# Linear attention and two feed-forward layers on one core: four blocks of the first layer turned into pairs of seven products, PReLU as one maximum, the whole kernel noted as one graph and ordered

## The chip, the cores and the metric

The kernel runs on one core of a Trainium2 chip. The metric is the time of one execution in device microseconds, as the median of several runs. The engines are named as in the profile: PE (TensorE), DVE (VectorE), ACT (ScalarE), POOL (GpSimd) and SP (SyncE, which here only issues DMAs).

## The reference

Linear attention comes first, then a feed-forward layer with PReLU, then one with a sigmoid gelu. All weights of the two feed-forward layers arrive as 64-bit floats and are turned into 32-bit ones on the chip.

```python
kv = np.einsum('bhsd,bhse->bhde', k, v)             # batch 8, heads 8, sequence 576, head size 64
out = np.einsum('bhsd,bhde->bhse', q, kv)
rms = np.sqrt(np.mean(out * out, axis=-1, keepdims=True) + 1e-06)
x = out / rms * g_norm                              # then laid out as 4608 tokens of 512 features
...
h = x @ w_in                                        # first layer: 512 -> 2048
g = np.maximum(h, 0.0) + alpha * np.minimum(h, 0.0)
x = g @ w_out                                       # 2048 -> 512
...
h = x @ w_in                                        # second layer, weights of its own
g = h * (1.0 / (1.0 + np.exp(-1.702 * h)))
return g @ w_out
```

## The kernel before, in words

The 4608 tokens are worked through in nine blocks of 512 tokens (j = 0 to 8). A feed-forward layer has 16 slices of 128 hidden features (m = 0 to 15). Each 32-bit operand is split into a high and a low part, and a product of two operands is three matmuls (high by high, high by low, low by high), each 128 by 128 by 512.

**Plain blocks.** `gemm_in` makes one slice h (12 matmuls), the activation makes g, `split` makes its two parts, and two steps later (`LAG`) `gemm_out` adds the slice to four output tiles y (12 matmuls). So a slice of a block is 24 matmuls and a block 384. All nine blocks of the first layer (l = 0) and block 0 of the second (l = 1) are plain. Blocks 0 and 1 of the first layer take turns, seven slices each first (`MH`), so that the weights have time to arrive; all 32 weight tiles of a layer stay in the on-chip memory.

**Pairs.** Blocks 1 and 2, 3 and 4, 5 and 6, 7 and 8 of the second layer are worked as pairs: two slices by two blocks are four hidden tiles, and a 2 by 2 scheme makes them from seven products instead of eight. A pair takes 7 x 8 = 56 steps (`NS`), and a step has 6 matmuls into the hidden tiles (`pair_in`) and 6 out of them (`pair_out`, 24 steps later, `LAGP`), so a pair is 672 matmuls. The price is sums and differences of blocks on DVE (`factor`), of weights beforehand on POOL (`w2_sums`), and a weight tile of 512 KB loaded from DRAM for each step (`weights`), since the prepared products are stored there.

**Weights.** `stage_words`, `stage_bits` and `stage_split` turn a loaded 64-bit weight into 32 bits (ACT two passes, DVE three, POOL one integer sum) and split it (ACT and DVE). For the second layer the products of two weight tiles at a time (one unit: k and kind, 16 in all) are made, split and stored to DRAM by `w2_steps`.

**Attention** of block j is made of small jobs (`job_kv`, `job_q`, `job_out`, `job_x`), spread by hand between the slices of block j-1. The PReLU reads the hidden tile in PSUM twice on DVE (lines 463 and 466); for seven slices of block 0 ACT makes two parts, and DVE joins them from the on-chip memory (line 459).

**Order.** Up to the pairs the order of instructions is written out by hand: `FIRST`, `ORDER` and `PROLOGUE` for the start, `jobs` by half steps for attention, `PREP` (half steps 44 to 280) for the second layer's weights. The pairs are noted as operations with costs, and `arrange` plays them through on a model and fixes the order on every engine.

Of the kernel before, what the change touches and what calls it, by code (L numbers as in the profile page):

```python
# [9 lines left out]
F32 = mybir.dt.float32  # L10
# [12 lines left out]
RING = 3  # L23
# [8 lines left out]
SEQ = "a0 a1 o0 a2 o1 . x0 o2 a3 x2 . o3 x1 . x3"  # L32

K1 = (0, 4)
J1 = (5, 9)
J2 = (3, 16)

RATE = (1.0, 0.55)


# [4 lines left out]
WA = 6  # L45
# [4 lines left out]
MM, TR, ACT, DVE, ISSUE, LAND, HOP = 0.2268, 0.09, 0.64, 0.71, 0.1, 4.5, 0.2  # L50
AHEAD = {"wt": 8.0, "xs": 20.0, "xc": 80.0, "gr": 8.0}
SLACK = 12.0
SPARE = (50.0, 4)

PREP = (44, 236)
# [4 lines left out]
def linear_attention_two_ffn_kernel(  # L60
# [22 lines left out]

    nc = tc.nc
# [14 lines left out]
    sp = ctx.enter_context(tc.tile_pool(name="small", bufs=2))  # L99

    big = ctx.enter_context(tc.tile_pool(name="big", bufs=1))
    half = ctx.enter_context(tc.tile_pool(name="half", bufs=1))
    n4 = [f"w{i}" for i in range(2 * M)]
    count = {"x": 2 * KC, "ld": RING, "raw": 1, "hl": LAG + 1}
    count2 = {"g": 1, "qT": 2, "xn": 2, "ev": 2, "da": 4, "dr": 2, "kR": 1, "vR": 1, "kv": 2}

    def place(tag, shape, dtype, name):
        if tag in count2:
            return half.tile(shape, dtype, tag=tag, name=name, bufs=count2[tag])
        return big.tile(shape, dtype, tag=tag, name=name, bufs=count.get(tag, 1))  # L110

    dram = ctx.enter_context(tc.tile_pool(name="dram", bufs=1, space=bass.MemoryType.DRAM))
    ps_h = ctx.enter_context(tc.tile_pool(name="ps_h", bufs=2, space=bass.MemoryType.PSUM))
    ps_y = ctx.enter_context(tc.tile_pool(name="ps_y", bufs=1, space=bass.MemoryType.PSUM))
    ps_a = ctx.enter_context(tc.tile_pool(name="ps_a", bufs=2, space=bass.MemoryType.PSUM))
# [3 lines left out]
    nalpha_sb = const.tile([P, M], F32, name="nalpha_sb")  # L119
    g_sb = const.tile([P, 1], F32, name="g_sb")  # L120
    kR = place("kR", [P, H, D], F32, "kR")
    vR = place("vR", [P, H, D], F32, "vR")
    kvb = [place("kv", [P, NP, P], F32, f"kv{i}") for i in range(2)]
# [5 lines left out]
    PAIRS = [(1, j) for j in range(1, NB, 2)]  # L129
    HB = TB // 2  # L130
    w2s = [dram.tile([P, 2, 2, HB], F32, name=f"w2s{u}") for u in range(NS)]
    ws = {1: w2s}
    src_d = {1: x2d}
    w2x = {kind: [dram.tile([P, 2, HB], F32, name=f"w2x{kind}{k}") for k in range(NQ)] for kind in ("wi", "wo")}


    loaded = {}
    queue = deque()

    def load(key, tag="ld"):  # L140
        t = place(tag, [P, 2 * TB], F32, "ld")
        LOAD[key[0]](t, *key[1:])
        loaded[key] = t

    def issue():
        if queue:
            load(queue.popleft())

    def runs(t0, n):
        done = 0  # L150
        while done < n:
            b, s = divmod(t0 + done, S)
            step = min(n - done, S - s)
            yield done, step, b, s
            done += step

    def load_q(t, i0):
        for e in range(2):
            for off, n, b, s in runs((i0 + e) * P, P):
                nc.sync.dma_start(  # L160
                    out=t[off : off + n, e * TB : (e + 1) * TB].rearrange("p (h d) -> p h d", h=H),
                    in_=q[b, :, s : s + n, :].rearrange("h p d -> p h d"),
                )

    def load_q0(t, p):
        for h in range(2):
            nc.sync.dma_start(
                out=t[:, 0:TB].rearrange("p (t h d) -> p t h d", h=2, d=D)[:, :, h, :],
                in_=q[0, 2 * p + h, 0:TB, :].rearrange("(t p) d -> p t d", p=P),
            )  # L170

    def load_kv(t, b, p):
        kt = t[:, 0:TB].rearrange("p (r h d) -> p r h d", r=R, h=2)
        vt = t[:, TB:].rearrange("p (h r d) -> p h r d", r=R, h=2)
        for h in range(2):
            nc.sync.dma_start(  # L176
                out=kt[:, :, h, :], in_=k[b, 2 * p + h, 0:S0, :].rearrange("(p r) d -> p r d", r=R)
            )
        nc.sync.dma_start(
            out=vt, in_=v[b, 2 * p : 2 * p + 2, 0:S0, :].rearrange("h (p r) d -> p h r d", r=R)  # L180
        )

    def load_rest(b):
        for t, src in ((kR, k), (vR, v)):
            nc.sync.dma_start(out=t[0:SR], in_=src[b, :, S0:S, :].rearrange("h p d -> p h d"))

    def load_win(t, l, m):
        nc.sync.dma_start(
            out=t.bitcast(I64).rearrange("p (c f) -> p c f", c=KC),
            in_=(w_in1, w_in2)[l][:, m * P : (m + 1) * P].rearrange("(c p) f -> p c f", p=P),  # L190
        )

    def load_wout(t, l, m):
        nc.sync.dma_start(out=t.bitcast(I64), in_=(w_out1, w_out2)[l][m * P : (m + 1) * P, :])

    def load_yp(t, c):
        nc.sync.dma_start(
            out=t.rearrange("p (c t) -> p c t", c=2), in_=yp[c : c + 2].rearrange("c p t -> p c t")
        )

    def load_x2(t, j, c):
        nc.sync.dma_start(
            out=t.rearrange("p (c t) -> p c t", c=2), in_=x2d[j][c : c + 2].rearrange("c p t -> p c t")
        )

    LOAD = {"q": load_q, "q0": load_q0, "kv": load_kv, "wi": load_win, "wo": load_wout, "x2": load_x2, "yp": load_yp}


    def split(src, hi, lo):
        nc.scalar.activation(out=hi, in_=src, func=AF.Copy)  # L210
        nc.vector.tensor_tensor(out=lo, in0=src, in1=hi.bitcast(F32), op=ALU.subtract)  # L211

    w_t = {}
    dec = {}

    def slot(kind, m):
        return n4[m + (M if kind == "wo" else 0)]

    def load_w(key):
        load(key, slot(key[0], key[2]))

    def stage_words(key):

        t = loaded[key]
        w2 = t.bitcast(U32).rearrange("p (n two) -> p n two", two=2)
        f2 = t.rearrange("p (n two) -> p n two", two=2)
        a = place("da", [P, TB], F32, "da")
        r = place("dr", [P, TB], I32, "dr")  # L230
        nc.scalar.activation(out=a, in_=f2[:, :, 1], func=AF.Abs)
        nc.scalar.activation(out=r, in_=w2[:, :, 0], func=AF.Copy, scale=2.0**-29)
        dec[key] = (a, r, w2[:, :, 1])

    def stage_bits(key):
        a, r, high = dec[key]
        au = a.bitcast(U32)

        nc.vector.tensor_scalar(out=a, in0=a, scalar1=2.0**-15, scalar2=122880.0, op0=ALU.max, op1=ALU.min)
        nc.vector.tensor_scalar(  # L240
            out=au,
            in0=au,
            scalar1=3,
            scalar2=0x3FFFFFF8,
            op0=ALU.logical_shift_left,
            op1=ALU.bitwise_and,
        )
        nc.vector.scalar_tensor_tensor(  # L248
            out=au, in0=high, scalar=0xC0000000, in1=au, op0=ALU.bitwise_and, op1=ALU.bitwise_or
        )  # L250
        ai = a.bitcast(I32)
        nc.gpsimd.tensor_tensor(out=ai, in0=ai, in1=r, op=ALU.add)  # L252

    def stage_split(key):
        a, _, _ = dec.pop(key)
        kind, l, m = key
        t = place(slot(kind, m), [P, 2, TB], F32R, "w")
        loaded.pop(key)
        split(a, t[:, 0, :], t[:, 1, :])
        w_t[key] = t  # L260


    def w2_load(kind, m):
        t = place("raw", [P, 2 * TB], F32, "raw")
        LOAD[kind](t, 1, m)
        loaded[kind, 1, m] = t

    def w2_place(kind, k, p):

        i = PRODUCTS.index(p)  # L270
        if kind == "wi":
            return w2s[k // 2 * 14 + 2 * i + k % 2][:, 0]
        return w2s[(k // SEG * 7 * SEG + i * SEG + k % SEG + LAGP) % NS][:, 1]

    def w2_out(src, dst):
        t = place("ev", [P, 2, HB], F32R, "wsp")
        split(src, t[:, 0, :], t[:, 1, :])
        nc.sync.dma_start(out=dst, in_=t.bitcast(F32))

    def w2_plain(kind, k, e):  # L280
        a = dec[kind, 1, 2 * k + e][0]
        loaded.pop((kind, 1, 2 * k + e))

        names = ((11, 12), (21, 22)) if kind == "wi" else ((11, 21), (12, 22))
        for h in range(2):
            name = names[e][h]
            dst = w2x[kind][k] if name == 21 else w2_place(kind, k, {11: 1, 12: 2, 22: 4}[name])
            w2_out(a[:, h * HB : (h + 1) * HB], dst)
# [835 lines left out]
```

## Time and profile before

| | us |
|---|---|
| median of 3 runs | 1676.7 (1676.02 to 1678.06) |
| the profiled execution | 1676.33 |
| span of its instructions | 1674.6 |
| PE busy in it | 1629.4 |

The profile is one execution. Busy time is that of each engine by itself; PEld is the weight load of PE, which runs beside its matmuls. In the rows by stage the columns are: stretch in us from the start, its length, then the busy time of PE, PEld, DVE, ACT and POOL with the number of instructions in brackets, the granted clock of PE as a share of full speed, the busy share of the DMA engines, and GB/s. The chain is followed back from the last instruction, at each step to what released it.

### The profile page before, as it was taken

How to read it: one execution, taken by the hardware profiler on the slowest of the kernel's cores; microseconds unless marked ns; L12 is line 12 of the kernel's file. 1: busy time of each engine (PE TensorE's matmuls, PEld its weight loads, DVE VectorE, ACT ScalarE, POOL GpSimd, SP SyncE). 2: the span in 40 equal slices, each digit the busy share in tenths (PEclk: the TensorE clock that was granted, in tenths of full speed). 3: DMA queues.
4: the chain of work that ended last, by engine and by line, in shares of the span. 5: the costliest groups of instructions: out<-in, count | busy, mean ns of one | idle time of the engine just before them, and what ended most of it. 6: DMA issues, size and time to landing. Idle time of an engine off the chain costs nothing.

```text
span 1674.6 us, 20949 instructions
## 1 busy us (share of the span) xinstructions
PE 1629.4 (97%) x7584; PEld 1346.5 (80%) x7584; DVE 1013.2 (61%) x1741; ACT 654.6 (39%) x1225; POOL 144.4 (9%) x138
## 2 busy tenths in 40 slices
PE   5889999999999999999999998999999999999998
PEld 4668877888888888888888887888888888888887
DVE  5888665655656566565656313476666648564555
ACT  4554332322322232233332223645455445544543
POOL 1323111110101111111111000000000000000000
PEclk8899999999999999999999999999999999999999
DMA  9750335333353432422238711757666756764752
GB/s 226 205 205 1 76 119 135 94 119 107 101 158 101 123 100 92 133 88 101 88 123 274 234 55 66 279 189 254 198 214 199 245 173 226 245 218 138 288 179 76
DMA packets 200535, 261.44 MB, mean 156 GB/s; under 512 B 92400, under 2 KB 133360, under 8 KB 200432
## 3 DMA queue, kind: packets, MB, share of 16 engines
q1 hardware_dynamic: 200432, 260.11, 48.6%
q8 instruction: 60, 0.98, 0.2%
q14 instruction: 43, 0.35, 0.1%
HBM read 206.58 MB, written 53.48 MB: 155 GB/s over the span
## 4 chain that ended last, share of the span: by engine, by line
PE 87%; DVE 4%; SPq 3%; DMA 2%; ACT 2%; issue 1%; POOL 0%; DVEq 0%; ACTq 0%; POOLq 0%
PE y L485 23%; PE cX L690 10%; PE V L690 10%; PE cZ L690 8%; PE W L690 8%; PE h L449 8%; PE h L451 8%; PE h L450 8%; PE ops L382 2%; SPq L176 1%; PE kvps L348 1%; SPq L160 1%; PE xTps L413 1%; PE oT L862 1%; PE qTps L372 1%
## 5 line engine op out<-in xcount | busy, mean ns | idle before, releaser
L485 PE MATMUL y<-gs,w 128*128 128x512 f32 x1728 | 427.3, 396 | 1.5 <-DVE ev L498 0.8
L485 PEld LDWEIGHTS y<-gs,w 128*128 128x128 f32 x1728 | 319.4, 189 | 68.7 <-DVE ev L498 1.7
L210 ACT ACTIVATE gs<-g 128x512 fp32r<-128x512 f32 x160 | 101.0, 632 | 430.7 <-DVE g L466 418.0
L449 PE MATMUL h<-x,w 128*128 128x512 f32 x640 | 256.3, 401 | 3.8 <-ACT x L415 3.7
L450 PE MATMUL h<-x,w 128*128 128x512 f32 x640 | 251.7, 393 | 0.1
L451 PE MATMUL h<-x,w 128*128 128x512 f32 x640 | 251.7, 393 | 0.0
L211 DVE TENSOR_TENSOR gs<-g,gs 128x512 fp32r<-128x512 f32 x160 | 113.7, 710 | 171.4 <-ACT gs L210 171.4
L690 PE MATMUL cX<-xc,wt 128*128 128x512 f32 x768 | 195.4, 391 | 4.4 <-DMA wt<-w2s 4.4
L690 PE MATMUL V<-gr,wt 128*128 128x512 f32 x768 | 195.6, 391 | 0.0
L690 PEld LDWEIGHTS cX<-xc,wt 128*128 128x128 f32 x768 | 144.9, 189 | 35.2 <-issue 4.8
L690 PEld LDWEIGHTS V<-gr,wt 128*128 128x128 f32 x768 | 142.9, 188 | 28.9
L463 DVE TENSOR_SCALAR g<-h,alpha_sb 128x512 f32<-128x512 f32 x137 | 102.4, 747 | 90.9 <-PE h L451 90.4
L252 POOL TENSOR_TENSOR da<-da,dr 128x512 int32<-128x512 int32 x64 | 91.2, 1425 | 765.6 <-DVE da L248 759.3
L690 PE MATMUL cZ<-xc,wt 128*128 128x512 f32 x576 | 146.5, 391 | 0.0
L690 PE MATMUL W<-gr,wt 128*128 128x512 f32 x576 | 145.1, 390 | 0.8 <-ACT ev L865 0.8
L449 PEld LDWEIGHTS h<-x,w 128*128 128x128 f32 x640 | 121.9, 190 | 28.9 <-ACT x L415 4.1
L451 PEld LDWEIGHTS h<-x,w 128*128 128x128 f32 x640 | 121.5, 190 | 26.0
L450 PEld LDWEIGHTS h<-x,w 128*128 128x128 f32 x640 | 121.9, 190 | 25.4 <-DVE x L416 1.1
L690 PEld LDWEIGHTS cZ<-xc,wt 128*128 128x128 f32 x576 | 109.1, 189 | 22.8
L690 PEld LDWEIGHTS W<-gr,wt 128*128 128x128 f32 x576 | 107.9, 188 | 23.8 <-ACT ev L865 1.5
L760 DVE TENSOR_TENSOR gr<-gt,gr 128x512 fp32r<-128x512 f32 x96 | 65.8, 688 | 56.7 <-ACT gr L756 55.3
L466 DVE SCALAR_TENSOR_TENSOR g<-h,g 128x512 f32<-128x512 f32 x137 | 94.7, 692 | 4.7
(99 smaller groups left out, 1718.8 us busy)
## 6 DMA issues: line engine op xcount, KB each, us to landing
wt<-w2s SPq DMA_DIRECT2D x200, 512.0 KB, 4.3
w2s<-wsp SPq DMA_DIRECT2D x112, 256.0 KB, 2.3
w<-w2s SPq DMA_DIRECT2D x48, 256.0 KB, 5.1
wt<-w2s SPq DMA_DIRECT2D x48, 256.0 KB, 3.8
x2d<-ev SPq DMA_DIRECT2D x36, 256.0 KB, 2.0
out_dram<-ev SPq DMA_DIRECT2D x36, 256.0 KB, 2.1
ld<-in_k_dram SPq DMA_DIRECT2D x64, 128.0 KB, 3.5
ld<-in_v_dram SPq DMA_DIRECT2D x32, 256.0 KB, 3.9
```

What stands on the lines that cost most here:

```text
L210: nc.scalar.activation(out=hi, in_=src, func=AF.Copy)
L211: nc.vector.tensor_tensor(out=lo, in0=src, in1=hi.bitcast(F32), op=ALU.subtract)
L252: nc.gpsimd.tensor_tensor(out=ai, in0=ai, in1=r, op=ALU.add)
L382: nc.tensor.matmul(ps[off : off + n, t], lhsT=qT[:, t * P + off : t * P + off + n], rhs=kvb[b % 2][:, p, :], start=True, stop=True,)
L449: nc.tensor.matmul(ps, lhsT=wh[:, c, :], rhs=x[c][:, 0], start=(c == 0), stop=False)
L450: nc.tensor.matmul(ps, lhsT=wh[:, c, :], rhs=x[c][:, 1], start=False, stop=False)
L451: nc.tensor.matmul(ps, lhsT=wl[:, c, :], rhs=x[c][:, 0], start=False, stop=(c == KC - 1))
L463: nc.vector.tensor_scalar(out=g, in0=ps, scalar1=0.0, scalar2=alpha_sb[:, m : m + 1], op0=ALU.min, op1=ALU.mult)
L466: nc.vector.scalar_tensor_tensor(out=g, in0=ps, scalar=0.0, in1=g, op0=ALU.max, op1=ALU.add)
L485: nc.tensor.matmul(y_t[c], lhsT=a, rhs=b, start=(m == m0 and n == 0), stop=(m == m1 and n == 2))
L690: nc.tensor.matmul(ps, lhsT=x, rhs=y, start=start and n == 0, stop=stop and n == 2, skip_group_check=True)
L760: nc.vector.tensor_tensor(out=t[:, 1], in0=val(), in1=t[:, 0].bitcast(F32), op=ALU.subtract)
```

## The change

- Blocks 5 to 8 of the first layer become two pairs (`run1`), of 56 steps each, with PReLU in place of gelu. Five blocks stay plain (`PLAIN`). The order of stages is: five plain blocks of the first layer, block 0 of the second layer, two pairs of the first layer, four pairs of the second.
- The attention of blocks 3 to 8 is now noted over 16 or 14 half steps each in place of 32 (`JOBS`), so that all of it is noted ahead of the end of block 4. The results of attention for blocks 3 to 8 are stored to DRAM (`xd`) and loaded again.
- The first layer's weights are needed twice: each is stored as 32 bits (`w1f`) when it has been converted, and three of its seven products are stored then; `weights1` loads the 32 bits again, makes the four other products on POOL (`sums`), splits them and stores them.
- PReLU is ACT's copy from PSUM with a sign (1 or -1, by whether alpha is at most 1), and then one instruction on DVE, the maximum of h and alpha times h, from and to the on-chip memory. The sign is multiplied into the second weights of the layer (`wo`).
- In a pair a step's weights come as two loads of 256 KB each (2 KB of each partition) and not as one of 512 KB.
- The hand order is gone. Every operation of the kernel is noted with its engine, cost, tiles and how far ahead it may start, `arrange` is run three times, each time with the PE starts of the run before as due times, and the best order is emitted. The model has POOL as an engine, a rate for the DMAs, and 1.7 times the cost for DVE operations marked `two` while POOL works. There are 45 tiles of 4 KB per partition and 20 of 2 KB for all.

```diff
-RING = 3
-FIRST = "qkrqkkqgwqkawwww"
-ORDER = "rkkkwwkwwqqw"
-PROLOGUE = "q0 k0 q1 o0 k1 o1 x0 q2 k2 o2 W B W k3 B e q3 x1 o3 S x2 W x3 B a W S S"
+FIRST = "q0 k0 q1 o0 k1 o1 x0 q2 k2 o2 k3 q3 x1 o3 x2 x3"
-J1 = (5, 9)
-J2 = (3, 16)
+J1 = (4, 9)
+J2 = (35, 16)
+PLAIN = 5
+JOBS = {3: (64, 16), 4: (80, 16), 5: (96, 16), 6: (112, 16), 7: (128, 14), 8: (142, 14)}
+PLAIN2_FIRST = True
-MM, TR, ACT, DVE, ISSUE, LAND, HOP = 0.2268, 0.09, 0.64, 0.71, 0.1, 4.5, 0.2
-AHEAD = {"wt": 8.0, "xs": 20.0, "xc": 80.0, "gr": 8.0}
-PREP = (44, 236)
+MM, TR, ACT, DVE, POOL, ISSUE, LAND, RATE, HOP = 0.2268, 0.09, 0.64, 0.71, 1.45, 0.65, 2.2, 0.3, 0.2
+AHEAD = {"wt": 10.0, "xs": 20.0, "xc": 80.0, "gr": 8.0, "ld": 14.0, "raw": 45.0, "w2p": 12.0, "x": 15.0}
+PASSES = 3
+RINGS = (6, 2, 3)
+N4, N2 = 45, 20
...
+    xd = {j: dram.tile([KC, P, TB], F32, name=f"xd{j}") for j in range(min(3, PLAIN), NB)}
...
+            if o.eng == "PE":
+                o.late = before[o.n] if before else o.clock
...
+            cost = o.cost
+            if o.two and free_at["POOL"] > t + 0.3:
+                cost *= 1.7
+            start[o.n] = t
+            free_at[o.eng] = t + cost
+            fin[o.n] = t + cost
+            if o.eng == "SP":
+                dma_at = max(dma_at, t + cost) + o.mb / RATE
+                fin[o.n] = dma_at + LAND
...
+    def emit():
+        found = None
+        starts = None
+        for _ in range(PASSES):
+            end, starts, fin = arrange(starts)
+            if found is None or end < found[0]:
+                found = (end, starts, fin)
...
+        for o in sorted(ops, key=lambda o: (starts[o.n], o.n)):
...
+        if j in xd:
+            xo = ("xo", j, p)
...
+                "SP", ISSUE, lambda: nc.sync.dma_start(out=xd[j][p], in_=tl(xo)), reads=[(xo, 0)],
...
+    def weight1(kind, m):
...
+        if kind == "wo":
+            note(
+                "ACT", ACT,
+                lambda: nc.scalar.activation(out=tl(da), in_=tl(da), func=AF.Copy, scale=sign_sb[:, m : m + 1]),
+                reads=[(("alpha",), 0)], writes=[(da, 0)], slack=None,
+            )
+        note_split([(da, 0)], lambda: tl(da), w, "halves", slack=None, held=[held_by[da]])
+        note(
+            "SP", ISSUE, lambda: nc.sync.dma_start(out=w1f[kind][m], in_=tl(da)), reads=[(da, 0), held_by[da]],
+            writes=[(("w1f", kind, m), 0)], slack=25.0, mb=0.26,
+        )
+        for h, pp in (((0, (1, 2)),), ((1, (4,)),))[m % 2] if kind == "wi" else (((0, (1,)),), ((0, (2,)), (1, (4,))))[m % 2]:
+            note(
+                "SP", ISSUE,
+                lambda h=h, pp=pp: nc.sync.dma_start(
+                    out=w_place(0, kind, m // 2, pp),
...
+    def sums(l, kind, k, da):
...
+        def one():
+            a11, a22, a12, a21 = parts()
+            t = tl(s12)
+            nc.gpsimd.tensor_tensor(out=t[:, 1], in0=a21, in1=a22, op=ALU.add)
+            nc.gpsimd.tensor_tensor(out=t[:, 0], in0=t[:, 1], in1=a11, op=ALU.subtract)
...
+        note("POOL", 1.8, one, reads=src, writes=[(s12, 0), t12], new=[(s12, [P, 2, HB], F32, "2")], **kw)
+        note("POOL", 1.8, two, reads=[*src, (s12, 0), t12], writes=[(s34, 0), t34], new=[(s34, [P, 2, HB], F32, "2")], **kw)
+    def weights1():
+        for k in range(NQ):
+            for kind in ("wi", "wo"):
...
+                        lambda da=das[e], src=w1f[kind][m]: nc.sync.dma_start(out=tl(da), in_=src),
...
+                sums(0, kind, k, das)
+    def prelu(o, m):
+        nc.vector.scalar_tensor_tensor(
+            out=o, in0=o, scalar=alpha_sb[:, m : m + 1], in1=o, op0=ALU.mult, op1=ALU.max
+        )
...
         def fn():
-            t = tl(("wt", u)).bitcast(F32)
-            if len(parts) == 2 and parts[0][1] is parts[1][1]:
-                nc.sync.dma_start(out=t, in_=parts[0][1])
-            else:
-                for e, w in parts:
-                    nc.sync.dma_start(out=t[:, e], in_=w[:, e])
+            t = tl(key).bitcast(F32)
+            for e, w in parts:
+                nc.sync.dma_start(out=t[:, e : e + 1], in_=w)
...
+        if not l:
+            note("DVE", DVE, lambda: prelu(val(), m), reads=[h], writes=[h], two=True)
...
-    segs += [(0, j, 0, M - 1) for j in range(2, NB)] + [(1, 0, 0, M - 1)]
+    segs += [(0, j, 0, M - 1) for j in range(2, PLAIN)]
...
+        plain(steps, jobs)
+        for fn in (weights2, weights1) if PLAIN2_FIRST else (weights1, weights2):
+            fn()
+        run1 = [(0, j) for j in range(PLAIN, NB, 2)]
+        run2 = [(1, j) for j in range(1, NB, 2)]
...
+        if PLAIN2_FIRST:
+            plain2()
+            pairs(run1 + run2)
```

## Rows read from the trace of the kernel before

**Rows 1.** The page: span, busy time of engines, chain that ended last.

```profile
span 1674.6 us, 20949 instructions
...
PE 1629.4 (97%) x7584; PEld 1346.5 (80%) x7584; DVE 1013.2 (61%) x1741; ACT 654.6 (39%) x1225; POOL 144.4 (9%) x138
...
PE 87%; DVE 4%; SPq 3%; DMA 2%; ACT 2%; issue 1%; POOL 0%; DVEq 0%; ACTq 0%; POOLq 0%
```

**Rows 2.** Busy time by stage: each engine, granted clock, DMA share, GB/s.

```profile
0.00:32.64 32.64, 17.56 (x104) 15.21 (x105) 15.41 (x39) 14.10 (x33) 5.24 (x12) 0.92 0.98 224
...
32.64:118.67 86.03, 71.16 (x317) 55.10 (x318) 68.33 (x120) 48.22 (x90) 25.06 (x16) 0.89 0.73 218
...
300.00:860.00 560.00, 559.85 (x2729) 465.31 (x2728) 352.23 (x656) 166.82 (x341) 70.97 (x73) 1.00 0.35 106
...
1028.80:1050.00 21.20, 16.78 (x64) 13.41 (x63) 5.58 (x9) 6.29 (x11) 0.00 (x0) 0.84 0.55 191
...
1050.00:1633.00 583.00, 582.23 (x2613) 481.87 (x2612) 354.81 (x554) 295.14 (x526) 0.00 (x0) 1.00 0.64 216
```

**Rows 3.** The chain in order of time: start us, us, what.

```profile
118.67 2.72 PE y L485 x12
...
358.69 2.72 PE y L485 x12
...
658.45 2.72 PE y L485 x12
...
1633.55 5.44 PE W L690 x24
```

**Rows 4.** What PE waited for: us in total, times, longest.

```profile
PE cX L690 <- DMA wt<-w2s: 4.4, 1, 4.4
```

**Rows 5.** Groups by line, DVE, ACT and POOL: busy us, mean ns, idle before.

```profile
L211 DVE TENSOR_TENSOR gs<-g,gs 128x512 fp32r<-128x512 f32 x160 | 113.7, 710 | 171.4 <-ACT gs L210 171.4
...
L463 DVE TENSOR_SCALAR g<-h,alpha_sb 128x512 f32<-128x512 f32 x137 | 102.4, 747 | 90.9 <-PE h L451 90.4
...
L466 DVE SCALAR_TENSOR_TENSOR g<-h,g 128x512 f32<-128x512 f32 x137 | 94.7, 692 | 4.7
...
L239 DVE TENSOR_SCALAR da<-da 128x512 f32<-128x512 f32 x64 | 29.7, 464 | 0.1
...
L240 DVE TENSOR_SCALAR da<-da 128x512 uint32<-128x512 uint32 x64 | 29.2, 457 | 2.2
...
L248 DVE SCALAR_TENSOR_TENSOR da<-raw,da 128x512 uint32<-128x512 uint32 x32 | 22.2, 692 | 1.1
...
L300 POOL TENSOR_TENSOR ws<-da,ws 128x256 f32<-128x256 f32 x16 | 14.0, 873 | 0.0
```

**Rows 6.** Line 459 by itself: duration ns min, median, max.

```profile
L459 DVE SCALAR_TENSOR_TENSOR g<-neg,nalpha_sb,g x7: 752/1528/1786, 39.1 to 99.3; 128x512 f32<-128x512 f32 x7
```

**Rows 7.** DVE in order of time: start us, us.

```profile
77.15 1.79 DVE L459 SCALAR_TENSOR_TENSOR g<-neg,nalpha_sb,g 128x512 f32<-128x512 f32 x1
```

**Rows 8.** POOL in order of time, the same stretch.

```profile
76.78 1.60 POOL L252 TENSOR_TENSOR da<-da,dr 128x512 int32<-128x512 int32 x1 [3.57 <-DVE da L248]
```

**Rows 9.** Busy time by stage again, a stretch of the start and one pair.

```profile
50.00:100.00 50.00, 40.77 (x195) 31.24 (x194) 44.10 (x82) 30.00 (x58) 15.50 (x10) 0.93 0.76 240
...
1100.00:1252.30 152.30, 152.06 (x687) 125.82 (x686) 96.52 (x150) 77.92 (x139) 0.00 (x0) 1.00 0.64 218
```

**Rows 10.** PE groups by line up to 118.67 us: count, busy us, mean ns.

```profile
L485 PE MATMUL y<-gs,w 128*128 128x512 f32 x85 | 21.6, 399 | 0.5 <-DVE w L211 0.5
...
L449 PE MATMUL h<-x,w 128*128 128x512 f32 x40 | 19.3, 483 | 3.8 <-ACT x L415 3.7
```

**Rows 11.** DMA issues: count, KB each, median us to landing.

```profile
w2s<-wsp SPq DMA_DIRECT2D x112, 256.0 KB, 2.3
...
raw<-in_moe_w_in_dram SPq DMA_DIRECT2D x16, 512.0 KB, 4.2
```

**Rows 12.** Tile wsp: its stores, min/median/max ns, first and last start us.

```profile
L278 SPq DMA_DIRECT2D w2s<-wsp x112: 319/338/1227, 230.9 to 928.5; - x112
```

More of the change, by code (lines that the diff above doesn't have):

```diff
@@ L98, in linear_attention_two_ffn_kernel @@
     const = ctx.enter_context(tc.tile_pool(name="const", bufs=1))
[L99 to L110, printed above, removed]
+    sp = ctx.enter_context(tc.tile_pool(name="small", bufs=8))
@@ L132, in linear_attention_two_ffn_kernel @@
[L132 to L155, printed above, removed]
@@ new lines, in arrange @@
+            cost = o.cost
[7 more added lines that the diff above has]
+                fin[o.n] = dma_at + LAND
+            changed = {o.eng}
+            if o.eng == "POOL":
+                changed.add("DVE")
+            for c, k in o.need:
+                del room[c][:k]
+                best.clear()
@@ L662, in pairs @@
-    def pairs():
+                    room[cls[key]].append(ends[key])
+                    room[cls[key]].sort()
+                    best.clear()
+            for a in after[o.n]:
+                left[a.n] -= 1
+                if not left[a.n]:
+                    arrive(a)
+                    changed.add(a.eng)
+            for e in changed:
+                best.pop(e, None)
+        for o in ops:
+            o.end = fin[o.n]
+        return max(s + o.cost for s, o in zip(start, ops) if o.eng == "PE"), start, fin
@@ new lines, in note_split, with part, value @@
+    def note_split(src, val, key, cost, ahead=None, slack=SLACK, low=None, dep=(), held=()):
+        halves = cost == "halves"
+        shape = [P, 2, 2, HB] if halves else [P, 2, TB]
+        def part(i):
+            return tl(key)[:, :, i] if halves else tl(key)[:, i]
+        def value():
+            return val().rearrange("p (h f) -> p h f", h=2) if halves else val()
+        note(
+            "ACT", ACT, lambda: nc.scalar.activation(out=part(0), in_=value(), func=AF.Copy), reads=src,
+            writes=[(key, 0), *dep], new=[(key, shape, F32R, "4")], ahead=ahead, slack=slack, low=low,
+        )
+        note(
+            "DVE", DVE,
+            lambda: nc.vector.tensor_tensor(out=part(1), in0=value(), in1=part(0).bitcast(F32), op=ALU.subtract),
+            reads=[*src, (key, 0), *held], writes=[(key, 1)], slack=slack, two=True,
+        )
@@ L726, in inputs @@
+                writes=[(key, e) for e in range(2)], new=[(key, [P, 2, TB], F32, "4")], ahead=AHEAD["xs"],
+                slack=None, low=SPARE, mb=0.52,
             )
@@ L878, in note_pairs, with pairs @@
+        note(
+            "ACT", ACT, lambda: nc.scalar.copy(tl(ev), tl(bank)), reads=[(bank, 0)], writes=[(ev, 0)],
+            new=[(ev, [P, TB], F32, "2")], slack=4.0,
+        )
+        note("SP", ISSUE, lambda: nc.sync.dma_start(out=out[r0 : r0 + P, :], in_=tl(ev)), reads=[(ev, 0)], mb=0.26)
+    def pairs(run):
+        n_in = len(run) * NS
+        pair_inputs(*run[0])
         for s in range(n_in + LAGP + 4):
             if s < n_in + LAGP:
-                weights(s)
-            if s < n_in and s % NS == NS // 2 and s // NS + 1 < len(PAIRS):
-                inputs(s // NS + 1)
+                pair_weights(run, s)
+            if s < n_in and s % NS == NS // 2 and s // NS + 1 < len(run):
+                pair_inputs(*run[s // NS + 1])
```

1357 lines of the change are left out of this document (673 added, 684 removed).

## The prediction

> **What bounds the kernel now.** The page comes first: PE is busy 97% of a span of 1674.6 us, DVE 61%, POOL 9%, and 87% of the chain that ended last is PE [rows 1]. A mean over stages can hide a stage that PE doesn't set, so the table by stage is next [rows 2]. From 300 to 860 us (plain blocks) PE is busy 559.85 of 560, and from 1050 to 1633 (pairs) 582.23 of 583, both at clock 1.00. In these two stages only fewer matmuls can save time. The chain gives the price of a matmul: 12 in 2.72 us in a plain block, 24 in 5.44 us in a pair [rows 3], so 0.2267 us in both. It also gives attention's part of PE: the same place of two blocks, three blocks apart, lies at 358.69 and 658.45, which is 99.9 us a block. A block has 384 matmuls, 87.0 us; 12.9 us are attention.
>
> What is not matmul time lies in two places. From 32.64 to 118.67 PE is busy 71.16 of 86.03 us at clock 0.89: 14.9 us idle and about 71.16 x 0.11 = 7.8 us of slow clock, 22.7 us that could at most come back. And where the second layer's plain block hands over to the pairs, PE waits 4.4 us for the first weight tile [rows 4]; 64 matmuls take 21.2 us there, where 64 x 0.2267 = 14.5 would do, so 6.7 us.
>
> **The change part by part, and the sum.**
>
> *Matmuls.* Four plain blocks are 4 x 384 = 1536 matmuls, two pairs are 2 x 672 = 1344. 192 less, x 0.2267 = 43.5 us. A stage that runs without a gap pays this in full; no transposes come with it, since the first layer's results are stored as they stand in the accumulators.
>
> *PReLU.* Lines 463 and 466 cost DVE 747 + 692 ns [rows 5], and now one instruction stands there. The nearest row is line 459, which also reads two on-chip tiles and a scalar of each partition: 752 ns at best, 1528 median, 1786 at most [rows 6]. The rows in order of time show what divides them: line 459 at 77.15 took 1.79 us, and POOL had an instruction of 1.60 us from 76.78 on [rows 7, 8]. So the price is 0.75 us alone and up to 1.79 beside POOL. ACT has one copy more for each slice, and for slices that were on ACT before one pass less; ACT is busy 167 of 560 us there [rows 2], so nothing.
>
> *The start.* From 50 to 100 us DVE is busy 44.1 of 50 [rows 9]: it sets the pace there. Line 459 saves 0.78 us (1528 to 752) in seven slices where it doesn't meet POOL, 5.4 us, and 0 where it always does; I take 3. Against it stand new stores. By the seventh slice 14 weights have been converted, with 14 stores of 0.26 MB in 32 bits and 7 x 3 products of 0.26 MB: 9.1 MB. The DMA engines move 240 GB/s at a share of 0.76 in this stretch, so 29 us of their time, and SP issues these stores in line with the loads. If they all went ahead of loads that PE waits for, 29 us. The DMA share falls to 0.35 later, and the stores have due times late enough to move there, so I take 0. Both ends stay in the range, as does the hand-written start giving back all its 22.7 us.
>
> *The shorter plain stage.* Work that was spread over 700 us must now fit from about 118 us to the first layer's pairs. Up to there 10 slices have gone in and 7 out (40 and 85 matmuls [rows 10]), 17 of the 160 halves of five plain blocks; the other 143 take 2.72 us each, 389. 7.5 blocks of attention add 97 us, and the second layer's plain block 87: 573 us. For DVE: a block of before has 352.23 x 99.9 / 560 = 62.8 us, of which 16 x (747 + 692 + 710) ns = 34.4 are PReLU and split [rows 5]; the other 28.4 are attention and the second layer's weights. Those are the same work as before, 7.2 blocks' worth, 205 us. To this come 71 slices x 1.46 = 104 us, 16 splits of the plain block 11, 32 splits of first-layer sums 23, about ten weights not yet converted at 2.3 us (464 + 457 + 692 + a split) 23, and 22 operations on the pair's inputs 15: 381 of 573 us, 66%. POOL gets about 42 integer sums of 1.6 us [rows 8] and 128 half sums of 873 ns at most [rows 5], 179 us. Even if each microsecond of POOL cost DVE another, 560 of 573 would be full. So 0, with little left over at the far end.
>
> *DMAs in that stage.* About 151 MB: second-layer weights 16.8, their eight products 33.6, first-layer 32-bit copies 16.8 written and read, products 29.4, attention 24, `xd` 8.4, results 5.2, weights of the plain block 16.8. That is 264 GB/s. At the shares of before the engines could move 106 / 0.35 = 303 and 216 / 0.64 = 338 GB/s [rows 2]. 78% to 87%: loads will land later than their 4.2 us [rows 11], but they are noted 10 to 45 us ahead. 0.
>
> *The first layer's pairs.* DVE is busy 96.5 of 152.3 us in a pair now [rows 9]. 32 PReLUs of 0.75 add 24: 79%. ACT loses the gelus (78 of 152 now). The loads are the same bytes in twice as many issues; a store's issue of this size took 338 ns [rows 12], and two of even 0.65 us fit in a step of 2.72. 0.
>
> *Hand-overs.* There are now two (into run 1 and out of the plain layer) in place of one of 6.7 us. One clean handover gains 6.7, one more loss costs 6.7; I take 0.
>
> The sum: 1676.3 - 43.5 - 3 = 1629.8, **1630 us**. The profiled execution is within 0.4 us of the median of the runs, so no other correction is due.
>
> One rule speaks against the new PReLU. The Trainium skill, "GPSIMD Engine Reference", section "1. Specifications", says that POOL shares its way into the on-chip memory with DVE, and that DVE instructions with two inputs from that memory contend for it. The trace agrees with it on line 459 (752 ns against 1786). By the rule every PReLU of the first layer's pairs is open to it, where lines 463 and 466 with one input were not; by the best row the sum stays 1630, by the rule at its worst it is rival 2, at up to 1681.
>
> **The rivals.**
>
> 1. *Part of the gain is lost at the start.* The stores wait on SP for a split, and loads stand behind them. For it: SP's order is fixed from a model that gives the DMAs 0.3 MB a us, and the first 32.64 us show 224 GB/s at a share of 0.98 [rows 2]. Against it: from 50 us on a quarter of the DMA time is free. Up to 29 us, with a second handover of 6.7 at most 36: 1633 + 15 to 36, 1648 to 1669.
>
> 2. *DVE sets the pace of the first layer's pairs.* The sums for the second layer's pairs aren't due until 305 us later, so the plan may leave them in run 1. Two pairs have 2 x 120.6 = 241 us of DVE work in 304.6; each us of POOL in there may cost DVE one. It decides from 64 us of POOL on; all 112 us of half sums would make 353, 48 us over: 1633 to 1681. Against it: the model puts work where an engine is free, and POOL is free in the plain stage.
>
> 3. *Slower: the on-chip tiles run out, and the second layer's weights come late.* While blocks 0 to 2 overlap, 32 weights, 8 inputs and 3 activations hold 43 of 45 large tiles, so the preparation can start only about slice 32. From there to the end of the plain block are 48 x 5.44 + 6.5 x 12.9 + 87 = 432 us. A unit holds two raw tiles for some 8 us (load 4.2, five passes) and four split tiles for some 5 us (a store lands in 2.3 [rows 11]): 36 tile-us, 576 for 16 units. With 6 free tiles it fits four times over; it decides below 576 / 432 = 1.33 tiles free on average. At the pace of before (stores from 230.9 to 928.5, 697.6 us [rows 12]) the last unit would be 265 us late. That pace was written by hand and had one raw tile, which speaks against it; at one tile free, 144 us late: 1777.
>
> 4. *Better than forecast.* The whole start runs dense, and the handovers too: 1633 - 22.7 - 6.7 = 1603.
>
> 5. *The ordering does nothing.* The steady stages leave 0.15 and 0.77 us of gaps; there the planner has nothing to win. This is already in the sum.
>
> **How the numbers follow.** Forecast (1611 to 1648) 0.62; better 0.10; rivals 1 and 2 short of the old time 0.13; about the old time 0.04; slower 0.11 (rival 3, and rival 2 at its end). Within 0.2% (3.4 us) is about what a measurement of this kernel can tell from no change. So faster 0.85, same 0.04, slower 0.11. The range from 1604 to 1670 leaves out half of the better case and the cases at or above the old time, 0.20 in all.
>
> **What would show it.** Right: PE without gaps in the first layer's pairs, 672 matmuls in 152.3 us, DVE near 79% there; PReLU at 0.75 us outside POOL's instructions. The matmuls in the profile fall by 192. Wrong: PE waiting for `wt`, `gr` or `w` in the plain stage or run 1; SP waiting on splits before 118 us; the first slice of the second layer's plain block waiting for its weight tile.

## The result and the profile after

The changed kernel takes 1609.8 us (median of 4 runs, 1609.13 to 1611.12) against 1676.4 for the kernel before beside it: ratio 0.9606 [0.9589, 0.9622], 66.6 us less. The forecast was 1630; the time lies in the wide range of 1604 to 1670, but 1.2 us below the 1611 to 1648 that the forecast gave itself as the likely case.

The page of the changed kernel, its span, busy times and the chain that ended last (answers to [rows 1]):

```profile
span 1607.6 us, 22206 instructions
...
PE 1577.5 (98%) x7392; PEld 1306.6 (81%) x7392; DVE 1124.7 (70%) x1793; ACT 807.5 (50%) x1431; POOL 212.6 (13%) x202
...
PE 94%; DVE 3%; DMA 1%; ACT 1%; issue 1%; SPq 0%; POOL 0%; ACTq 0%; DVEq 0%
```

PE has 192 matmuls less, as counted, and is now 94% of the chain instead of 87%.

The busy times by stage, with the columns of [rows 2, 9]: the start, its middle, then the plain stage (to the first matmul of a pair at 671.7 us), 100 us out of it, 87 us near its end, the first layer's two pairs, and one pair's length out of these:

```profile
32.64:118.67 86.03, 74.21 (x336) 56.66 (x335) 81.02 (x134) 60.61 (x105) 26.85 (x18) 0.92 0.85 282
50.00:100.00 50.00, 41.57 (x184) 30.42 (x183) 46.28 (x84) 35.44 (x64) 15.20 (x10) 0.87 0.74 272
118.67:671.70 553.03, 552.79 (x2777) 461.45 (x2776) 400.15 (x654) 294.10 (x520) 181.79 (x173) 1.00 0.83 269
200.00:300.00 100.00, 100.00 (x500) 83.04 (x499) 77.26 (x124) 53.91 (x94) 35.84 (x34) 1.00 0.79 249
570.00:657.00 87.00, 87.00 (x385) 72.06 (x384) 28.41 (x40) 30.62 (x52) 16.64 (x19) 1.00 1.01 368
671.70:976.30 304.60, 304.60 (x1346) 252.21 (x1345) 236.75 (x361) 131.05 (x225) 0.00 (x0) 1.00 0.70 227
700.00:852.30 152.30, 152.30 (x674) 126.11 (x673) 120.69 (x184) 65.54 (x113) 0.00 (x0) 1.00 0.62 198
```

From 118.67 to 1562 us PE idles 1.1 us in all; 5.3 more lie in the last 45.6 us, where the output is written. DVE is at 72% in the plain stage (400.15 of 553.03) and at 79% in a pair (120.69 of 152.30), and PE doesn't wait for it.

What PE waited for from 118 us to the end, the whole answer (line, releaser, us in total, times, longest):

```profile
PE W L770 <- ACT ov L1077: 0.9, 3, 0.3
```

The wait for the first weight tile of the pairs [rows 4] is gone, and no wait at either hand-over is left in this list.

**Where 67 us came from.** The PE groups of the feed-forward up to 118.67 us, where [rows 10] had 205 matmuls (85, and three lines of 40):

```profile
L770 PE MATMUL h<-x,w 128*128 128x512 f32 x132 | 35.0, 407 | 3.4 <-DVE w L554 1.8 <-ACT g L797 0.8 <-ACT x L531 0.8
L770 PE MATMUL y<-gs,w 128*128 128x512 f32 x108 | 29.9, 422 | 1.2 <-DVE gs L554 1.2
```

Now 240 are done at this point, and attention's 216 matmuls are the same number in both. From there to the end the two kernels compare as follows; first the kernel before, with two stretches in which it lost time and its longest wait in the first of them, then the changed kernel:

```profile
118.67:1674.60 1555.93, 1540.71 (x7164) 1276.16 (x7163) 929.51 (x1582) 592.27 (x1104) 114.09 (x110) 1.00 0.47 151
200.00:300.00 100.00, 95.22 (x468) 78.30 (x467) 58.51 (x111) 28.47 (x58) 10.90 (x12) 0.98 0.41 122
960.00:1050.00 90.00, 85.58 (x367) 70.40 (x366) 25.22 (x40) 26.60 (x45) 0.00 (x0) 0.96 0.22 77
```

```profile
PE xTps L413 <- DVE xn L406: 2.1, 1, 2.1
```

```profile
118.67:1607.60 1488.93, 1482.52 (x6937) 1231.28 (x6935) 1030.73 (x1624) 733.23 (x1296) 181.79 (x173) 1.00 0.72 233
```

The stretch is 67.0 us shorter and has 7164 - 6937 = 227 matmuls less. Of these 192 are the pairs', 43.5 us at 0.2267, and 35 were done earlier, 7.9 us. Of the other 15.6, 8.8 are waits: PE idles 15.22 us before and 6.41 after. The last 6.8 are matmuls that took less time. The granted clock accounts for some 4.2 of these: it was 0.98 from 200 to 300 us (0.02 x 95.22 = 1.9), and 0.84 at the hand-over (16.78 us in [rows 2] for 64 matmuls that take 14.5 without a gap, 2.3); it is 1.00 in the changed kernel's stages after 118.67. The remaining 2.6 were not traced.

**PReLU.** The new line by itself, in the plain blocks and in the pairs (duration in ns min, median, max, first and last start):

```profile
L734 DVE SCALAR_TENSOR_TENSOR g<-g,alpha_sb x80: 737/750/1854, 44.6 to 577.6; 128x512 f32<-128x512 f32 x80
L734 DVE SCALAR_TENSOR_TENSOR gt<-gt,alpha_sb x32: 743/752/754, 676.9 to 939.3; 128x512 f32<-128x512 f32 x32
L734 DVE SCALAR_TENSOR_TENSOR gl<-gl,alpha_sb x32: 744/752/755, 685.1 to 944.7; 128x512 f32<-128x512 f32 x32
```

0.75 us as forecast, and up to 1.85 in the stage in which POOL works. In the pairs none is longer than 0.755, and POOL is at 0.00 us there.

### The profile page after: what moved, and what is told of

It is laid out like the page before. It is cut to its first block, busy times and chain, and to the rows that moved or that the text cites. A ratio compares the mean times of both kernels' runs of the same rounds, so it can differ in the third digit from the quotient of the medians.

```text
span 1607.6 us, 22206 instructions
## 1 busy us (share of the span) xinstructions
PE 1577.5 (98%) x7392; PEld 1306.6 (81%) x7392; DVE 1124.7 (70%) x1793; ACT 807.5 (50%) x1431; POOL 212.6 (13%) x202
## 4 chain that ended last, share of the span: by engine, by line
PE 94%; DVE 3%; DMA 1%; ACT 1%; issue 1%; SPq 0%; POOL 0%; ACTq 0%; DVEq 0%
PE V L770 16%; PE X L770 16%; PE y L770 15%; PE h L770 15%; PE W L770 12%; PE Z L770 12%; PE ops L453 2%; PE kvps L371 2%; PE xTps L506 1%; PE qTps L437 1%; DMA w0wi<-w 1%; PE oT L1070 1%; PE kvps L373 0%; DVE w L554 0%; DMA vR<-in_v_dram 0%
## 5 line engine op out<-in xcount | busy, mean ns | idle before, releaser
L770 PE MATMUL V<-gr,wt 128*128 128x512 f32 x1152 | 293.0, 391 | 0.0
L770 PE MATMUL X<-xc,wt 128*128 128x512 f32 x1152 | 291.2, 389 | 0.0
L770 PE MATMUL h<-x,w 128*128 128x512 f32 x1152 | 287.0, 397 | 3.4 <-DVE w L554 1.8
L770 PEld LDWEIGHTS X<-xc,wt 128*128 128x128 f32 x1152 | 216.2, 188 | 45.1
L770 PEld LDWEIGHTS h<-x,w 128*128 128x128 f32 x1152 | 211.8, 188 | 49.6 <-DVE w L554 3.5
L770 PE MATMUL y<-gs,w 128*128 128x512 f32 x960 | 240.4, 399 | 1.2 <-DVE gs L554 1.2
L770 PE MATMUL Z<-xc,wt 128*128 128x512 f32 x864 | 218.4, 389 | 0.0
L770 PEld LDWEIGHTS y<-gs,w 128*128 128x128 f32 x960 | 177.7, 190 | 37.3 <-DVE gs L554 1.5
L770 PEld LDWEIGHTS Z<-xc,wt 128*128 128x128 f32 x864 | 162.2, 188 | 33.7
L554 DVE TENSOR_TENSOR gr<-gl,gr 128x512 fp32r<-128x512 f32 x144 | 98.7, 687 | 47.8 <-ACT gr L549 47.5
```

The lines of the kernel that those rows point to most:

```text
L554: lambda: nc.vector.tensor_tensor(out=part(1), in0=value(), in1=part(0).bitcast(F32), op=ALU.subtract),
L770: nc.tensor.matmul(o, lhsT=x, rhs=y, start=start and n == 0, stop=stop and n == 2, skip_group_check=True)
```

## The experiments

Experiments 1, 2, 3 and 5 tell the parts of the change apart (the order, the PReLU, the pairs); the others try the rivals. They ran on several chips, each beside the kernel before, so the ratio to that kernel is the better comparison; the difference of two ratios is known to some 3 us. And wherever an edit changes what `arrange` plans, the whole order is made anew: orders of the same work differ by up to 9 us (experiments 9 and 12), so a few us between two planned kernels can't be put down to the edit alone.

**1. The order alone, all nine blocks plain, attention noted as in the kernel before.** The maximum for PReLU is in it too.

```
-PLAIN = 5
+PLAIN = 9
-JOBS = {3: (64, 16), 4: (80, 16), 5: (96, 16), 6: (112, 16), 7: (128, 14), 8: (142, 14)}
+JOBS = {j: (64 + 32 * (j - 3), 31) for j in range(3, 9)}
...
-        for fn in (weights2, weights1) if PLAIN2_FIRST else (weights1, weights2):
+        for fn in (weights2,):
```

The stores of `w1f` and of the three products in `weight1` are left out as well, since nothing reads them.

> All nine blocks of the first layer stay plain, attention is spread over 32 half steps a block again, the first layer's products and 32-bit copies are not made; order and PReLU are those of the new kernel. Theory A (192 matmuls are 43.5 us, and the other 23 us come from the ordering of the whole kernel): 1653 us, within 4, and PE waits only in the first 105 us. Theory B (the ordering wins nothing in stages that were dense already; the rest comes with the pairs): 1670 to 1677 us.

1666.4 us, ratio 0.9959 [0.9946, 0.9971]: a small gain, which lies between the two theories. The start is as good as in the changed kernel (247 feed-forward matmuls by 118.67 us), but it has a stall that neither the kernel before nor the changed one has in this place. What PE waited for from 290 to 420 us, and 100 us of that by engine:

```profile
PE h L756 <- DVE x L554: 3.3, 1, 3.3
PE xTps L506 <- DVE xn L483: 3.1, 1, 3.1
PE h L756 <- ACT x L549: 2.4, 1, 2.4
```

```profile
300.00:400.00 100.00, 91.15 (x427) 74.96 (x426) 88.20 (x124) 57.02 (x101) 49.79 (x42) 0.95 0.84 276
```

POOL is busy half of this time and DVE 88%: it seems that preparation of the second layer's weights lies close together here, and that attention's chain through DVE comes late. Experiment 5, with attention in other places, doesn't have the stall; the cause was not tried further.

**2. PReLU alone, in the kernel before.**

```
-            neg = place("ev", [P, TB], F32, "neg")
-            nc.scalar.activation(out=neg, in_=ps, func=AF.Relu, scale=-1.0)
-            nc.scalar.activation(out=g, in_=ps, func=AF.Relu)
+            nc.scalar.copy(g, ps)
             nc.vector.scalar_tensor_tensor(
-                out=g, in0=neg, scalar=nalpha_sb[:, m : m + 1], in1=g, op0=ALU.mult, op1=ALU.add
+                out=g, in0=g, scalar=alpha_sb[:, m : m + 1], in1=g, op0=ALU.mult, op1=ALU.max
             )
```

and the same copy and maximum in place of lines 463 and 466 for the other slices.

> The kernel before with one edit: ACT copies the hidden tile, one maximum on DVE makes PReLU. Theory A (PReLU is off the path but in the start): 1671 to 1677 us, of the start's 85 us at most 5 back. Theory C (the PReLU relieves DVE and that is what shortens the start and the 201 to 300 us stage): 1655 to 1662 us.

1673.1 us, ratio 0.9996 [0.9987, 1.0005]: no difference. DVE's busy time falls from 1013.2 to 948.2 us and buys nothing, as theory A had it. In the middle of the start it doesn't even fall:

```profile
50.00:100.00 50.00, 40.14 (x192) 30.73 (x190) 44.41 (x80) 26.38 (x52) 15.97 (x10) 0.93 0.77 246
```

DVE 44.41 us against 44.10 in [rows 9]: the 3 us of relief that the forecast took there are not to be had this way. The maximum in the seven slices of line 459 shows why:

```profile
L457 DVE SCALAR_TENSOR_TENSOR g<-g,alpha_sb x7: 743/1753/1784, 38.4 to 98.2; 128x512 f32<-128x512 f32 x7
```

Its median is 1753 ns where line 459 had 1528 [rows 6]. It too reads two on-chip tiles, and is long as often as the instruction that it replaces.

**3. The changed kernel with the two-step PReLU in its plain blocks.**

```
+        def two_steps():
+            nc.vector.tensor_scalar(
+                out=tl(g), in0=tl(bank), scalar1=0.0, scalar2=alpha_sb[:, m : m + 1], op0=ALU.min, op1=ALU.mult
+            )
+            nc.vector.scalar_tensor_tensor(out=tl(g), in0=tl(bank), scalar=0.0, in1=tl(g), op0=ALU.max, op1=ALU.add)
...
-            note("DVE", DVE, lambda: prelu(tl(g), m), reads=[(g, 0)], writes=[(g, 0)], two=True)
```

> The new kernel with the two DVE instructions from PSUM as PReLU in its plain blocks (the pairs keep the maximum). DVE gets about 80 x (1.44 - 0.91) = 43 us more, from 77% to some 86% of the plain stage. Theory A: 1609 to 1614 us, what is added lies in the start. Theory C: 1620 us or more.

1607.3 us, ratio 0.9602 [0.9589, 0.9615], which by the ratio is the same as the changed kernel (0.9606); the time itself is 1.7 us below theory A's range. By 118.67 us 248 matmuls are done. In the plain blocks too the form of PReLU gains nothing that these runs can tell from zero. With experiment 2 this holds for the hand order and for a planned one.

**4. The product stores held back.**

```
-                reads=[(w, 0), (w, 1)], ...
+                reads=[(w, 0), (w, 1), (("w1done",), 0)], ...
```

> The new kernel, but the stores of the first layer's products wait until all 32 weights are converted, so none of these 40 stores lies in the start. If stores ahead of loads cost time in the start (rival 1 of the prediction): 1600 to 1606 us. If DVE sets the pace there and the stores lie beside it: 1608 to 1612 us.

1678.7 us, ratio 1.0041 [1.0027, 1.0054], some 70 us over the changed kernel. But the edit isn't what the expectation says. Each conversion writes the same token, so each had to wait for the stores of the weight before it. POOL's integer sums, one for each weight, then stand far apart (start, us, then in brackets the idle time ahead and its releaser):

```profile
67.79 1.26 POOL L612 TENSOR_TENSOR da<-da,dr__695 128x512 int32<-128x512 int32 x1 [14.72 <-ACT dr__695 L592]
...
80.65 1.30 POOL L612 TENSOR_TENSOR da<-da,dr__769 128x512 int32<-128x512 int32 x1 [11.60 <-ACT dr__769 L592]
```

It answers another question: a chain of store, landing and conversion for each weight costs as much as the whole change gained. On the stores' own cost it says nothing; experiment 7 does.

**5. All nine blocks plain, attention noted as in the changed kernel.** As experiment 1, with `JOBS` left as they are in the change.

> As the first experiment (no first-layer pairs, no work for them), but attention keeps the places that it has in the new kernel, so that the first 80 steps have the same jobs. If the pairs are worth their 192 matmuls and nothing else: 43.5 us above the new kernel, 1651 to 1655 us. If the stall of the first experiment (PE waiting for block 3's inputs between 340 and 364 us) comes again without the pairs' work: 1662 to 1670 us.

1655.0 us, ratio 0.9885 [0.987, 0.9899], 19.6 us below the kernel before on the same chip. Its span is 45.3 us above the changed kernel's (46.8 us by the two ratios, as the runs are of different chips). 43.5 of that are the 192 matmuls, and PE's waits from 118.67 us on are some 2 us more; the start is the same (241 matmuls by 118.67 us). So within some 3 us the pairs gain their matmuls and nothing else, and the order with the earlier attention gains 19.6 us by itself. Against experiment 1, only where attention is noted differs: 11.7 us of span. Experiment 1 and this one from 118.67 us to their ends, one execution each:

```profile
118.67:1664.60 1545.93, 1529.86 (x7122) 1269.28 (x7121) 871.53 (x1372) 688.38 (x1195) 133.50 (x109) 1.00 0.51 163
```

```profile
118.67:1652.90 1534.23, 1526.20 (x7129) 1267.89 (x7127) 860.92 (x1373) 688.68 (x1196) 128.52 (x109) 1.00 0.51 165
```

The kernel before has 1555.93 us and 7164 matmuls there. Experiment 5 is 21.7 us shorter with 35 matmuls less (7.9), so some 14 us of waits and slow matmuls are gone without any pair. Experiment 1 is 10.0 us shorter with 42 less (9.5): hardly anything is left, although from 201 to 300 us and from 960 to 1050 PE is without a gap in it (99.00 of 99 and 90.00 of 90 us). Its new stall costs what these two stretches give back.

**6. One pair in place of two.**

```
-PLAIN = 5
+PLAIN = 7
```

> The new kernel with blocks 5 and 6 plain and one first-layer pair (7, 8). 96 matmuls more than the new kernel: 21.8 us, 1629 to 1633 us if matmuls are all; 1640 us or more if a hand-over or a stall goes with the number of pairs.

1625.7 us, ratio 0.9713 [0.9698, 0.9727], 15.9 us over the changed kernel (17.9 by the ratios) where 96 matmuls are 21.8, and below the range that was expected. The difference lies in the start: 150 + 120 = 270 matmuls by 118.67 us, 30 more than the changed kernel, 6.8 us. 21.8 - 6.8 = 15.0.

```profile
L770 PE MATMUL h<-x,w 128*128 128x512 f32 x150 | 39.3, 408 | 4.0 <-ACT w L549 2.4 <-DVE w L554 1.6
L770 PE MATMUL y<-gs,w 128*128 128x512 f32 x120 | 31.7, 413 | 3.5 <-ACT w L549 2.1 <-DVE w L554 1.4
```

**7. The product stores truly behind the start.** They are taken out of `weight1` and noted in `weights1`, unit by unit, each also reading the token that the conversions of the first layer write.

```
+    def product_stores(kind, m):
...
+                reads=[(w, 0), (w, 1), (("w1done",), 0)],
...
             for kind in ("wi", "wo"):
+                for e in range(2):
+                    product_stores(kind, 2 * k + e)
```

> The new kernel with the 40 product stores of the first layer noted behind the last conversion, so that they are not in line with the conversions (the fourth experiment tied each conversion to the stores before it, which was not meant). If stores ahead of loads cost time in the start (rival 1 of the prediction): 1600 to 1606 us. If they lie beside DVE's work: 1608 to 1612 us.

1610.4 us, ratio 0.9619 [0.9605, 0.9634]: the same. The start without these stores:

```profile
32.64:118.67 86.03, 75.44 (x341) 58.71 (x342) 81.95 (x137) 59.07 (x104) 25.78 (x18) 0.92 0.68 208
```

The DMAs move 208 GB/s here in place of 282, so (282 - 208) x 86.03 us = 6.4 MB are gone from the start, and by 118.67 us 241 feed-forward matmuls are done in place of 240. The 32-bit copies are still stored in the start here; experiment 5, which has neither kind of store, has 241 as well. The stores lie beside other work.

**8. Three pairs.** Three plain blocks; attention of blocks 3 to 6 noted in 11 or 10 half steps each, that of 7 and 8 inside the first pairs.

```
-PLAIN = 5
+PLAIN = 3
+JOBS = {3: (51, 11), 4: (62, 11), 5: (73, 11), 6: (84, 10)}
+PAIR_JOBS = {7: (0, 27), 8: (28, 27)}
```

> Three first-layer pairs (blocks 3 to 8), attention of blocks 7 and 8 inside the first of them. If matmuls are all: 21.8 us less than the new kernel, 1588 us. If the preparation of weights needs the room of five plain blocks (rival 3 of the prediction, one step further): 1640 us or more, with PE waiting for weights in the second layer's plain block.

1681.5 us, ratio 1.0041 [1.0027, 1.0055]: 96 matmuls less than the changed kernel, and a little slower than the kernel before. Three stretches with losses, and PE's longest waits from 118 us on:

```profile
200.00:300.00 100.00, 74.31 (x336) 60.21 (x337) 73.64 (x122) 49.09 (x88) 42.05 (x39) 0.83 0.76 240
500.00:600.00 100.00, 78.55 (x348) 63.87 (x347) 60.48 (x93) 39.43 (x69) 29.05 (x36) 0.88 0.95 301
600.00:700.00 100.00, 90.71 (x399) 73.39 (x399) 76.26 (x129) 49.64 (x91) 16.48 (x20) 0.90 0.87 300
```

```profile
PE X L771 <- DMA wt<-w0wi: 8.9, 2, 8.3
PE qTps L438 <- DVE xn L484: 8.0, 3, 3.9
PE X L771 <- issue: 7.7, 1, 7.7
```

The waits were expected in the second layer's plain block and lie elsewhere: in the denser attention from 200 us on, and at the start of the first pairs, where weight tiles come late with the DMAs at a share of 0.95. The edit shortens the stage and packs attention at once, so it doesn't say which of the two sets the limit; it says only that a third pair doesn't pay with attention placed like this.

**9. Another order of the same operations.** `arrange` runs three times; the change emits the order that its model likes best, here the first. This one emits the third.

```
-            if found is None or end < found[0]:
-                found = (end, starts, fin)
+            found = (end, starts, fin)
```

> The new kernel, but the order of the third pass of the planner is emitted and not the one that ends first on its model (in the kernel with one pair the third pass was emitted, and 270 matmuls of the feed-forward were begun by 118.67 us where the new kernel had 240). If the pass is what differs in the start: about 270 here too, 30 x 0.2267 = 6.8 us less, 1601 to 1605 us. If the model's choice holds on the chip: 1612 us or more.

1604.2 us (1603.9 to 1605.85), ratio 0.9585 [0.9572, 0.9598], the fastest version here. It wasn't run beside the changed kernel on one chip, and the two intervals overlap (0.9606 [0.9589, 0.9622] there), so the runs alone don't show that it is faster. The traces, one execution each, point that way: the span is 1602.2, 5.4 us less, and by 118.67 us 147 + 120 = 267 matmuls are done, 27 more, 6.1 us. Experiment 6's order was a third run's as well, and has a better start too.

**10. Experiment 9 with the two-step PReLU of experiment 3.**

> The third pass's order with the two-step PReLU of the third experiment in the plain blocks. If PReLU is off the path in either order: within 3 us of the run with the last pass alone.

1606.3 us, ratio 0.9598 [0.9585, 0.9611]. 2.1 us over experiment 9 on the same chip, within the 3 that were expected, and the intervals of the ratios overlap. So for the third time PReLU's form makes no difference of more than 2 us or so.

**11. 43 tiles of 4 KB in place of 45.**

```
-N4, N2 = 45, 20
+N4, N2 = 43, 20
```

> The new kernel with 43 tiles of 4 KB in place of 45. If room is what the preparation of weights lives on (rival 3 of the prediction): 1625 us or more, PE waiting for weights or inputs in the plain stage. If there is room to spare: within 3 us of 1609.8.

1620.0 us, ratio 0.9676 [0.9663, 0.969], 10 us more (11.7 by the ratios), between the two theories. PE's waits from 118 us on, as far as they are new:

```profile
PE h L770 <- ACT x L549: 2.3, 1, 2.3
PE X L770 <- ACT gt L1005: 1.8, 1, 1.8
PE xTps L506 <- DVE xn L483: 1.3, 2, 0.7
PE h L770 <- DVE x L554: 1.1, 1, 1.1
```

The preparation moves back (POOL still works after 700 us, where the changed kernel's is done before the pairs), and small waits appear. That is about 5 us a tile, though some of it may be the luck of another order. It fits rival 3's tiles running short, but not so short that weights come late.

**12. The model without POOL's price for DVE.**

```
-                cost *= 1.7
+                cost *= 1.0
```

> The new kernel ordered by a model in which DVE operations beside POOL cost what they cost alone (factor 1.0 for 1.7). If the factor matters: 5 us or more above the new kernel, with PE waiting for DVE in the plain stage, where POOL is busiest. If PE has slack enough: within 3 us.

1613.6 us, ratio 0.964 [0.9627, 0.9653], by the ratios 5.7 us over the changed kernel (3.8 by the times), and 9.4 over experiment 9 on the same chip. The start is better (156 + 120 = 276 matmuls), the rest is worse. PE's waits from 118 us on:

```profile
PE xTps L506 <- DVE xn L483: 6.1, 5, 2.4
PE ops L453 <- ACT qT L441: 3.0, 1, 3.0
```

This fits the reading that attention's chain through DVE is planned too tightly where the order is made as if DVE kept its speed beside POOL. It is one order for each model, though, so it isn't shown that the factor made the difference.

## Why the prediction was right, and where it was wrong

**Matmuls, -43.5: right.** The count fell by 192, a pair's 672 matmuls take 152.3 us without a gap, and experiment 5 against the changed kernel gives 45.3 us (46.8 by the ratios) with about 2 of waits.

**The start, -3: right in sign, wrong in its reason and its size.** It gave 7.9 us, and not by PReLU: experiments 2, 3 and 10 find nothing in that. The forecast took line 459's best duration for the new instruction in slices that don't meet POOL, but the maximum meets POOL as often (median 1753 ns in experiment 2). What changes from order to order is how many matmuls are done by 118.67 us, from 240 to 276 with the same work. The sum's other term here, 0 for the stores, was right: in experiment 7 the product stores are gone, in experiment 5 the 32-bit copies too, and the start stays the same. One of the signs of being wrong did show, SP waiting on splits before 118 us (line 649 of the changed kernel issues the product stores; us in total, times, longest):

```profile
SPq L649 <- DVE w L554: 14.9, 7, 4.9
```

By the two experiments it cost nothing, so rival 1's wait is real and its price falls.

**The plain stage, 0: right, and close in its parts.** It is 553 us long where 573 were worked out: 8 us of its matmuls were done at the start already, and of its 2777 matmuls 712 are attention's, which took 552.8 - 2065 x 0.2267 = 84.7 us in place of 97. With the 216 of the start nine blocks have 928, 103 each, so 6.9 blocks of attention were left and not the 7.5 of the sum. DVE has 400 us of work where 381 were forecast, 72% and not 66%, and POOL 182 where 179 were. The DMAs move 269 GB/s at a share of 0.83, as forecast (264 at 0.78 to 0.87).

**The pairs, 0: right.** DVE has 120.69 us of work in one, where 96.5 + 24 were forecast. POOL has nothing left to do there, so rival 2 did not come about. The Trainium skill, "GPSIMD Engine Reference", section "1. Specifications", says that DVE instructions with two on-chip inputs contend with POOL, which spoke against the change there. The trace agrees with it: PReLU with two on-chip inputs takes from 737 to 1854 ns in the stage in which POOL works, and at most 755 here, where it doesn't. It just finds no POOL work to contend with in this stage.

**Hand-overs, 0, and "the ordering does nothing": this is the step that failed.** After the start 15.6 us were gained that the sum doesn't have. The prediction says that what is not matmul time "lies in two places", the start and one hand-over, and, from the stretches 300 to 860 and 1050 to 1633, that "there the planner has nothing to win". There was a third place: from 200 to 300 us PE was busy 95.22 of 100 us at a clock of 0.98, with its waits inside attention's chain. This stretch, 4.8 us idle and 1.9 of slow clock, stands in the sum at nothing and without a reason. The hand-over, 4.4 us of wait and 2.3 of clock, was priced rightly at 6.7, but the sum took 0 for it where all of it came back. These two are 13.4 of the 15.6 us; the rest, with some small waits, was not traced.

Experiment 5 shows that it was not the pairs: order and attention's new places alone give some 14 us after the start. Experiment 1 shows that the planned order doesn't do it with attention in the old places: it closes both stretches and opens a stall elsewhere. So what won was the order together with attention's places. Which part closed the hand-over isn't told apart from the two smaller weight loads in each step, which every planned version has.

Together the two terms are 7.9 - 3 + 15.6 = 20.5 us, the 20 by which the forecast was too high. That the time lies in the range all the same is owed to the part of rival 4 that the range took in. Rival 4 came nearest, but not for its reasons alone: its 6.7 us for the hand-over came, of its 22.7 for the start a third, and the stretch from 200 to 300 us it didn't have.

**Rival 3** did not come about. Two tiles less (experiment 11) cost some 10 us and not the 144 that it gave for a late preparation; how much of that is the tiles and how much another order is not shown.

Two more things stay open. Why one order does 240 matmuls by 118.67 us and another 276 was not followed to one operation: DVE has 46.28 of 50 us in the middle of the changed kernel's start, so which of its operations goes first may matter there, but no experiment moved one alone. And which resource stops the third pair (experiment 8) isn't told apart.

## What to carry to other kernels

Before a hand order is called dense, every stretch of the busy table needs its price, the short ones between the long dense ones too: here 13.4 us lay in two of them, and the sum had one at 0 and the other not at all. Time taken off an engine isn't time off the kernel: 65 us less of DVE made no difference that the runs could tell. And a machine-made order is worth trying in more than one variant on the chip, since orders of the same work, 1604.2 us in experiment 9 and 1613.6 in experiment 12 on the same chip, differed by 9.4 us, and by the traces the one that the model preferred was not the fastest.

## What the runs showed of the hardware

In two places of the trace POOL seems to hold back more on DVE than operations with two large inputs. DVE and then POOL in order of time in the changed kernel (start, us):

```profile
92.57 1.00 DVE L477 TENSOR_TENSOR sa<-sa,sr 128x8 f32<-128x8 f32 x1
...
98.52 1.39 DVE L599 TENSOR_SCALAR da<-da 128x512 uint32<-128x512 uint32 x1
```

```profile
91.90 1.65 POOL L612 TENSOR_TENSOR da<-da,dr__910 128x512 int32<-128x512 int32 x1 [5.39 <-DVE da L606]
...
98.28 1.34 POOL L612 TENSOR_TENSOR da<-da,dr__948 128x512 int32<-128x512 int32 x1 [4.73 <-DVE da L606]
```

An operation on 8 elements of each partition, 0.168 us at the median, took 1.00 us and ended at 93.57, where POOL's ended at 93.55; one with a single input, 0.428 at the median, took 1.39 and ended at 99.91, 0.29 us after POOL's (99.62). So it seems that a short DVE operation can cost about what is left of POOL's instruction; no experiment took the POOL instruction away to see.

And from 570 to 657 us, most of it the second layer's plain block, PE ran 87.00 of 87.00 us while the DMAs moved 368 GB/s at a share of 1.01: in this stretch full DMA engines cost PE nothing, since it waited for nothing that they brought.
